# Which engine makes the last copy and issues the final store of a decode layer

## The chip, the cores and the metric

The kernel runs on one core of a Trainium2 chip. The metric is the device time of one execution in microseconds (us). The profile of an execution also gives a *span*, from the kernel's first recorded instruction to its last. The span is about 2 us shorter than the time. That difference matters in this study, and is called "time less span" below.

A ratio is the mean time of one kernel's fast runs over that of the kernel before's fast runs of the same rounds, so it is not quite the ratio of the medians that stand beside it.

The engines named below have these parts in this kernel. TensorE makes the matrix products, whose sums lie in the memory called PSUM. VectorE and ScalarE compute on elements and copy sums from PSUM to SBUF, the working memory. SyncE issues DMA transfers. A semaphore is a counter that an engine or a transfer raises and that another engine waits for. SPq and ACTq in the profile are the instruction queues of SyncE and ScalarE.

## The reference

The reference is one decode step of a transformer layer: four sequences, one token each, width 1024.

```python
x = A_x
h = x + _A_ref(_layernorm(x), A_k_cache, A_v_cache, A_wq, A_wo)   # attention, the last 2048 keys
h2 = h + _B_ref(_layernorm(h), B_w1, B_w3, B_w2)                   # silu(gate) * up, then w2
return h2                                                          # 4 x 1 x 1024, bf16
```

It reads 55.6 MB of weights and cache and writes 8 KB.

## The kernel before

All large loads are issued by SyncE in the order of a plan, through five buffers. `load_rows` cuts a tile into pieces, one load each. Each load takes the next of eight completion semaphores in turn ("lane" 0 to 7).

```python
def load_rows(src, n, r0, pieces):
    t = stream.tile([P, SLOT], BF16, tag="s")
    i = 0
    for m in pieces:
        nc.sync.dma_start(out=t[:, i * n : (i + m) * n], in_=src[:, (r0 + i) * n : (r0 + i + m) * n])
        i += m
    return [t[:, k * n : (k + 1) * n] for k in range(i)]

plan = (
    [("wq", load_rows, (wq_v, N_Q, c, [2, 2] if c == 0 else [4])) for c in range(0, KC, RQ)]
    # ... k, v, wo, w1 ...
    + [("w3", load_rows, (w3_v, N_F, c, [RQ])) for c in range(0, KC, RQ)]
    + [("w2", load_rows, (w2_v, D, 0, [16])), ("w2", load_rows, (w2_v, D, 16, [5, 4, 2, 1]))]
)
```

ScalarE issues five small loads of x at the start, then works as one of the two engines that copy out of PSUM:

```python
nc.scalar.dma_start(out=x_sb[:], in_=x_flat)
load_next(5)
# ...
for j in range(JG):                       # JG = 4
    nc.scalar.dma_start(out=x_q[QD * j : QD * (j + 1) : RS, :], in_=x_flat[:, j * CG : (j + 1) * CG])
```

The end of the kernel: 112 matmuls accumulate the last product as w2 arrives, VectorE casts the sum from PSUM to SBUF, and SyncE issues the store. Only 16 of the 128 partitions hold results.

```python
for i in range(IF):                       # IF = 28 rows of w2
    for j in range(JG):
        nc.tensor.matmul(y2_ps[QD * j : QD * (j + 1), :], lhsT=hgT[:, i, :],
                         rhs=loaded["w2"][i][:, j * CG : (j + 1) * CG], ...)
res = act.tile([P, CG], BF16)             # 128 x 256
nc.vector.tensor_copy(out=res[:], in_=y2_ps[:])
nc.sync.dma_start(out=out_flat.rearrange("b (j c) -> j b c", j=JG), in_=res[0:P:RS, :])
```

After that the compiler adds a wait of SyncE for all engines and all eight lanes, and two barriers.

Of the kernel before, what the change touches and what calls it, by code (L numbers as in the profile page):

```python
# [10 lines left out]
P = 128  # L11
# [8 lines left out]
def kernel(  # L20
# [13 lines left out]
    nc = tc.nc  # L34

    B, _, D = A_x.shape
    Hkv, Sk, Dh = A_k_cache.shape[1], A_k_cache.shape[2], A_k_cache.shape[3]
    Hq = A_wq.shape[1] // Dh
    REP = Hq // Hkv
    W = min(4096, max(256, Sk // 4))  # L40
    F = B_w1.shape[1]
    KC = D // P
    FC = F // P
    NK = W // P
    NSB = W // 512
    assert B == 4 and D == KC * P and F == FC * P and Hq * Dh == 4096
    assert Dh == P and W == NK * P and B * Hq == P and Hkv == 4
    eps = 1e-5
    qscale = float(Dh) ** -0.5
# [2 lines left out]
    out_flat = out.flatten_outer_dims()  # L52
# [14 lines left out]
    JG = 4  # L67
    QD = P // JG
    RS = QD // B
# [89 lines left out]
    for j in range(JG):  # L159
        nc.scalar.dma_start(  # L160
            out=x_q[QD * j : QD * (j + 1) : RS, :], in_=x_flat[:, j * CG : (j + 1) * CG]
# [7 lines left out]
    for c in range(2):  # L169
# [8 lines left out]
        out=xn[:], in0=x_sb[:], scalar1=mv[:, 0:1], scalar2=rstd[:, 0:1],  # L178
# [4 lines left out]
    for kc in range(KC):  # L183
# [15 lines left out]
        out=perm[:].rearrange("p (h dq) -> p h dq", dq=JG),  # L199
        in_=ident[:].rearrange("p (dq h) -> p h dq", dq=JG),  # L200
# [7 lines left out]
    for j in range(2, JG):  # L208
        nc.vector.tensor_tensor(
            out=same[:, 0, :], in0=same[:, 0, :], in1=ident[:, j * QD : (j + 1) * QD], op=ALU.add  # L210
# [24 lines left out]
    for r in range(REP):  # L235
        nc.tensor.transpose(out=qt_ps[:, r, :], in_=q_sb[:, r * Dh : (r + 1) * Dh], identity=ident[:])  # L236
    nc.vector.tensor_copy(
        out=qz[:, :, : Hkv * QD].rearrange("p b (g z) -> p b g z", g=Hkv)[:, :, :, :REP],
        in_=qt_ps[:].rearrange("p r (g x) -> p x g r", g=Hkv)[:, :B, :, :],
# [24 lines left out]
    for u, (b, n) in enumerate(units):  # L264
        k_v = loaded["k"][b].rearrange("p (j d) -> p j d", d=Dh)
        kT = ktpool.tile([P, NJ, P], BF16, tag="kT")
        for t in range(NJ // TB):
            kt_ps = psA.tile([P, TB, P], BF16, tag=f"kt{nt % 4}")
            for jj in range(TB):
                nc.tensor.transpose(  # L270
                    out=kt_ps[:, jj, :], in_=k_v[:, n * NJ + t * TB + jj, :], identity=ident[:]
# [23 lines left out]
        out=Pm[:].rearrange("q (c jq) -> q jq c", jq=NSB), in_=scores_ps[:].rearrange("q (jq c) -> q jq c", jq=NSB),  # L295
# [48 lines left out]
    y2_ps = psB.tile([P, CG], FP32, tag="y2")  # L344
    g_ps = psB.tile([P, 2, 512], FP32, tag="g")
    u_ps = psB.tile([P, 2, 512], FP32, tag="u")
    for i in range(IO):
# [33 lines left out]
        out=hn[:], in0=h1[:], scalar1=tot[:, 0:1], scalar2=rstd2[:, 0:1],  # L381
# [5 lines left out]
        out=hnT[:].rearrange("p k x -> p (k x)"), in_=hn[:].rearrange("q (c k) -> q k c", k=KC)  # L387
# [5 lines left out]
    def gate_up(kind, out_ps):  # L393
# [27 lines left out]
        out=hgT[:].rearrange("p i x -> p (i x)"),  # L421
        in_=hg[:].rearrange("q s c -> q (s c)").rearrange("q (c i) -> q i c", i=IF),
# [12 lines left out]
            )  # L435

    res = act.tile([P, CG], BF16)
    nc.vector.tensor_copy(out=res[:], in_=y2_ps[:])  # L438
    nc.sync.dma_start(out=out_flat.rearrange("b (j c) -> j b c", j=JG), in_=res[0:P:RS, :])


# [28 lines left out]
```

## Time and profile before

| | before |
|---|---|
| time | 139.43 us median (139.16 to 139.54, 6 runs) |
| span of the profiled run | 137.42 us |
| TensorE / VectorE / ScalarE busy | 52% / 26% / 21% |
| DMA | 55.6 MB, mean 406 GB/s |

These lines are from the page of the kernel before. The first two are the span and the busy time of each engine; the DMA line is the busy share of the 16 DMA engines in 40 slices of the span, in tenths; the queue lines give packets, MB and share of DMA time (q1 is SyncE's queue, q10 ScalarE's).

```profile
span 137.4 us, 2307 instructions
...
PE 71.2 (52%) x1045; PEld 45.2 (33%) x1045; DVE 36.3 (26%) x63; ACT 29.0 (21%) x28; POOL 1.6 (1%) x7
...
DMA  5999999999999999999999999999999999998950
...
q1 hardware_dynamic: 4724, 55.58, 95.4%
...
q10 hardware_dynamic: 40, 0.02, 0.0%
...
DMA 70%; PE 19%; ACT 6%; SPq 1%; DVE 1%; issue 1%; ACTq 0%
```

The DMA row is at 8 tenths or more from the second slice until the last two, and the last line, the chain of work that ended last, is 70% DMA. So the load stream bounds the kernel. Only what comes after the last load can shorten the time without making the stream faster.

The end of that chain, in order of time (start, length, what):

```profile
95.17 37.81 DMA t<-in_B_w_dram
...
133.02 1.04 PE y_ps L428 x9
...
134.09 0.42 DVE res L438
```

The timeline of the tail (start, length, engine, line, operation; in brackets how long the engine had been idle and what ended that):

```profile
133.02 1.02 PE L428 MATMUL y_ps<-t,hgT 128*32 128x256 bf16 x12 [0.32 <-DMA t<-in_B_w_dram]
...
134.09 0.42 DVE L438 CAST res<-y_ps 128x256 bf16<-128x256 f32 x1 [11.51 <-PE y_ps L428]
134.54 0.70 SPq L439 DMA_DIRECT2D out_dram<-res  x1
```

The instructions that touch res, with their durations in ns, and SyncE's waits for the copy and for the store's landing:

```profile
L438 DVE CAST res<-y_ps x1: 425/425/425, 134.1 to 134.1; 128x256 bf16<-128x256 f32 x1
L439 SPq DMA_DIRECT2D out_dram<-res x1: 697/697/697, 134.5 to 134.5; - x1
```

```profile
SPq L439 <- DVE res L438: 34.9, 1, 34.9
...
SPq L465 <- DMA out_dram<-res: 1.1, 1, 1.1
```

From the last matmul on, everything is serial. One thing follows another: copy 0.42 us, issue 0.70 us, landing about 1.1 us, and 1.07 us until the span ends.

For the cost of the copy on ScalarE, its own groups by shape give two durations (count, busy us, mean ns):

```profile
L276 ACT COPY kT<-kt_ps 128x1024 bf16<-128x1024 bf16 x16 | 15.8, 1014 | 12.0 <-PE kt_ps L270 12.0
...
L314 ACT CAST PT_sb<-pt_ps 128x512 bf16<-128x512 f32 x2 | 1.2, 585 | 2.0 <-PE pt_ps L308 2.0
```

### The profile page before, as it was taken

The page shows a single profiled execution, that of the slowest core. Times are in us where ns is not written, and L with a number is a line of the kernel's source. Part 1 is how long each engine was busy: PE and PEld are TensorE (multiplying, and loading weights), DVE is VectorE, ACT ScalarE, POOL GpSimd, SP SyncE. Part 2 cuts the span into 40 slices and gives each one's busy share as a digit, 9 for nine tenths or more (in the row PEclk, how much of TensorE's full clock was granted, in tenths as well). Part 3 has the DMA queues.
Part 4 walks back from the last instruction along what each step waited for, and adds up shares of the span by engine and source line. Part 5 has one row for each costly group of instructions (what it writes and reads, how often), then busy time and mean ns, then how long its engine had stood idle before and what let it go on. Part 6 is the DMA issues. An engine that isn't in the chain of part 4 may idle for free.

```text
span 137.4 us, 2307 instructions
## 1 busy us (share of the span) xinstructions
PE 71.2 (52%) x1045; PEld 45.2 (33%) x1045; DVE 36.3 (26%) x63; ACT 29.0 (21%) x28; POOL 1.6 (1%) x7
## 2 busy tenths in 40 slices
PE   0152304798989889100995579544090530802960
PEld 0110001175656565000894457221030210302830
DVE  6430000244444444601400300530003970160001
ACT  0400000155564646098610000000005000000000
POOL 4000000000000000000000000000000000000000
PEclk9999999999999999975555555558655586555555
DMA  5999999999999999999999999999999999998950
GB/s 155 444 402 520 391 391 444 420 429 444 405 440 392 421 421 414 423 495 476 401 391 424 453 428 397 459 467 401 409 459 439 426 409 430 448 458 359 420 217 2
DMA packets 4773, 55.74 MB, mean 406 GB/s; under 512 B 376, under 2 KB 408, under 8 KB 2716
## 3 DMA queue, kind: packets, MB, share of 16 engines
q1 hardware_dynamic: 4724, 55.58, 95.4%
q8 instruction: 8, 0.13, 0.3%
q10 hardware_dynamic: 40, 0.02, 0.0%
q14 instruction: 1, 0.01, 0.0%
HBM read 55.59 MB, written 0.01 MB: 405 GB/s over the span
## 4 chain that ended last, share of the span: by engine, by line
DMA 70%; PE 19%; ACT 6%; SPq 1%; DVE 1%; issue 1%; ACTq 0%
DMA t<-in_B_w_dram 54%; DMA t<-in_A_wq_dram 15%; PE kt_ps L270 9%; ACT kT L276 5%; PE scores_ps L255 5%; PE q_ps L222 3%; PE g_ps L398 2%; SPq L97 1%; PE y_ps L428 1%; DVE q_sb L232 1%; ACT q_sb L233 0%; DVE res L438 0%; PE qt_ps L236 0%; ACTq L276 0%
## 5 line engine op out<-in xcount | busy, mean ns | idle before, releaser
L276 ACT COPY kT<-kt_ps 128x1024 bf16<-128x1024 bf16 x16 | 15.8, 1014 | 12.0 <-PE kt_ps L270 12.0
L270 PE MATMUL kt_ps<-ident,t 128*128 128x128 bf16 x256 | 16.5, 219 | 0.0
L270 PEld LDWEIGHTS <-t 128*128 128x128 bf16 x256 | 14.4, 98 | 5.0 <-issue 4.9
L274 DVE COPY kT<-kt_ps 128x1024 bf16<-128x1024 bf16 x16 | 11.1, 692 | 15.2 <-PE kt_ps L270 15.2
L398 PEld LDWEIGHTS <-hnT 128*32 128x32 bf16 x128 | 5.5, 140 | 25.0 <-issue 22.7
L222 PE MATMUL q_ps<-t,xnT 128*4 128x512 bf16 x64 | 7.2, 615 | 12.0 <-DMA t<-in_A_wq_dram 12.0
L398 PE MATMUL u_ps<-t,hnT 128*32 128x448 bf16 x64 | 6.4, 576 | 10.6 <-DMA t<-in_B_w_dram 10.6
L255 PE MATMUL scores_ps<-kT,qz 128*32 128x512 bf16 x64 | 9.9, 609 | 3.1 <-ACT kT L276 3.1
L428 PE MATMUL y_ps<-t,hgT 128*32 128x256 bf16 x112 | 6.7, 415 | 7.6 <-DMA t<-in_B_w_dram 7.6
L398 PE MATMUL g_ps<-t,hnT 128*32 128x448 bf16 x64 | 6.3, 574 | 8.0 <-DMA t<-in_B_w_dram 8.0
L322 PE MATMUL OT_ps<-PT_sb,t 128*128 128x8 bf16 x256 | 7.4, 168 | 1.9 <-issue 1.7
L428 PEld LDWEIGHTS <-hgT 128*32 128x32 bf16 x112 | 4.8, 139 | 10.0 <-issue 5.5
L349 PE MATMUL y_ps<-t,o 128*32 128x256 bf16 x128 | 7.2, 418 | 1.7 <-DMA t<-in_A_wo_dram 0.9
L322 PEld LDWEIGHTS <-t 128*128 128x128 bf16 x256 | 7.3, 104 | 2.1 <-issue 2.0
L222 PEld LDWEIGHTS <-xnT 128*4 128x4 bf16 x64 | 2.0, 111 | 16.4 <-issue 16.1
L308 PE MATMUL pt_ps<-Dm,Pm 128*128 128x128 bf16 x16 | 1.9, 308 | 9.3 <-DVE Dm L301 9.3
L349 PEld LDWEIGHTS <-o 128*32 128x32 bf16 x128 | 5.1, 144 | 3.5 <-issue 1.2
L412 DVE RECIPROCAL eg<-eg 128x896 f32<-128x896 f32 x1 | 5.8, 5754 | 0.0
L232 DVE TENSOR_SCALAR q_sb<-q_ps 128x512 bf16<-128x512 f32 x1 | 0.7, 692 | 17.8 <-PE q_ps L222 17.8
L233 ACT ACTIVATE q_sb<-q_ps 128x512 bf16<-128x512 f32 x1 | 0.6, 597 | 21.4 <-DVE q_sb L232 21.4
L308 PEld LDWEIGHTS <-Pm 128*128 128x128 bf16 x16 | 1.6, 142 | 9.8 <-ACT Pm L294 9.8
L294 ACT ACTIVATE Pm<-scores_ps,nmax 128x2048 bf16<-128x2048 f32 x1 | 4.8, 4783 | 0.0
(67 smaller groups left out, 37.0 us busy)
## 6 DMA issues: line engine op xcount, KB each, us to landing
t<-in_B_w_dram SPq DMA_DIRECT2D x4, 3584.0 KB
t<-in_A_k_cache_dram SPq DMA_DIRECT2D x4, 2048.0 KB, 25.6
t<-in_A_v_cache_dram SPq DMA_DIRECT2D x4, 2048.0 KB, 33.0
t<-in_A_wo_dram SPq DMA_DIRECT2D x2, 4096.0 KB, 32.5
t<-in_A_wq_dram SPq DMA_DIRECT2D x2, 2048.0 KB, 9.6
t<-in_A_wq_dram SPq DMA_DIRECT2D x1, 4096.0 KB, 21.0
t<-in_B_w_dram SPq DMA_DIRECT2D x1, 4096.0 KB, 39.9
t<-in_B_w_dram SPq DMA_DIRECT2D x1, 1280.0 KB, 34.9
```

The lines of the kernel that those rows point to most:

```text
L222: nc.tensor.matmul(q_ps[QD * g : QD * g + B, hf * 512 : (hf + 1) * 512], lhsT=xnT[:, kc, :], rhs=wq_t[:, c0 : c0 + 512], start=(kc == 0), ...
L255: nc.tensor.matmul(scores_ps[QD * g : QD * (g + 1), n * 512 : (n + 1) * 512], lhsT=qz[:, b, g * QD : (g + 1) * QD], rhs=kT_v[:, g, :, :], ...
L270: nc.tensor.transpose(out=kt_ps[:, jj, :], in_=k_v[:, n * NJ + t * TB + jj, :], identity=ident[:])
L274: nc.vector.tensor_copy(out=kT[:, t * TB : (t + 1) * TB, :], in_=kt_ps[:])
L276: nc.scalar.copy(out=kT[:, t * TB : (t + 1) * TB, :], in_=kt_ps[:])
L294: nc.scalar.activation(out=Pm[:].rearrange("q (c jq) -> q jq c", jq=NSB), in_=scores_ps[:].rearrange("q (jq c) -> q jq c", jq=NSB), func=A ...
L308: nc.tensor.matmul(pt_ps[:, jj, :], lhsT=Pm[:, (jb * JPB + jj) * P : (jb * JPB + jj + 1) * P], rhs=Dm[:], start=True, stop=True)
L322: nc.tensor.matmul(OT_ps[:, b, g * REP : (g + 1) * REP], lhsT=v_t[:, g, j, :], rhs=PT_sb[:, j, g * QD + b * REP : g * QD + (b + 1) * REP], ...
L349: nc.tensor.matmul(y_ps[QD * j : QD * (j + 1), :], lhsT=o4[:, i, :, :].rearrange("p b s -> p (b s)"), rhs=loaded["wo"][i][:, j * CG : (j + ...
L398: nc.tensor.matmul(out_ps[QD * j : QD * (j + 1), hf, :HF], lhsT=hnT[:, k, :], rhs=loaded[kind][k][:, c0 : c0 + HF], start=(k == 0), stop=( ...
L412: nc.vector.reciprocal(out=eg[:], in_=eg[:])
L428: nc.tensor.matmul(y2_ps[QD * j : QD * (j + 1), :], lhsT=hgT[:, i, :], rhs=loaded["w2"][i][:, j * CG : (j + 1) * CG], start=False, stop=(i ...
```

## The change

The intent is to keep copy and store on one engine: ScalarE reads PSUM, and issues the store itself, so no other engine has to be told. (An assertion on a shape is rewritten as well, which changes no instruction.)

```diff
     res = act.tile([P, CG], BF16)
-    nc.vector.tensor_copy(out=res[:], in_=y2_ps[:])
-    nc.sync.dma_start(out=out_flat.rearrange("b (j c) -> j b c", j=JG), in_=res[0:P:RS, :])
+    nc.scalar.copy(out=res[:], in_=y2_ps[:])
+    nc.scalar.dma_start(out=out_flat.rearrange("b (j c) -> j b c", j=JG), in_=res[0:P:RS, :])
```

The built program differs in nothing else: VectorE loses one instruction, SyncE the store, ScalarE gains both, with no table load.

More of the change, by code (lines that the diff above doesn't have):

```diff
@@ L42 @@
     KC = D // P
-    FC = F // P
     NK = W // P
     NSB = W // 512
-    assert B == 4 and D == KC * P and F == FC * P and Hq * Dh == 4096
+    assert B == 4 and D == KC * P and F % P == 0 and Hq * Dh == 4096
     assert Dh == P and W == NK * P and B * Hq == P and Hkv == 4
```

## The prediction

> **What bounds the kernel.** The DMA load stream. The page has the 16 DMA engines 90% busy or more in nearly all of the 40 slices, at a mean of 406 GB/s for 55.6 MB. The chain that ended last is 70% DMA; its last links are a 37.8 us load that ends at 132.98 us, 1.04 us of y_ps matmuls, and the 0.42 us copy to res. TensorE is busy 52%, VectorE 26%, ScalarE 21%. The built program keeps the order of instructions on every engine except for the two moved ones, so nothing before the last matmul should change.
>
> **What moves: the tail.** After the last matmul everything is serial and critical (timeline of the tail, and the queue's waits; span 137.42 us):
>
> - last y_ps matmul ends, about 134.04; copy on VectorE 134.09 to 134.51 (0.425 us);
> - store issued by SyncE 134.54 to 135.24 (0.697 us);
> - SyncE's wait for the store to land: 1.1 us, to 136.35;
> - end of the program, 1.07 us: SyncE checks the remaining semaphores, the engines meet in two barriers.
>
> The change touches 0.425 + 0.03 + 0.697 = 1.15 us. If all of it vanished, the gain would be 0.8%: beyond 2% is out of reach.
>
> **Costs.**
> 1. Copy. ScalarE's PSUM to SBUF cast of 128x512 takes 585 ns, its copy of 128x1024 1014 ns: 0.84 ns an element (of different types), so 128x256 should take about 0.37 us (estimate), 0.05 less than VectorE. The Trainium skill, "ScalarE: Activation LUTs", section "What ACT_TABLE_LOAD costs", states 0.833 ns an element; these lines agree. The built program has no table load for the copy.
> 2. Hop. VectorE to SyncE took 0.03 us. ScalarE still waits on its own completion semaphore before it issues: 0.03 to 0.07 us, so "same engine" saves about nothing.
> 3. Issue. ScalarE's five issues took 0.56 to 0.68 us (four-row transfers); SyncE's unobstructed loads 0.33 to 0.64, its store 0.70. I expect 0.6 to 0.9 us on ScalarE: -0.1 to +0.2.
> 4. Flight. The same 8 KB goes through the same 16 DMA engines, idle by then. The Trainium skill, "DMA: Bandwidth & Descriptors", section "Issuing engines are not separate DMA queues", says that only sequencer issue time is saved. ScalarE's load of x_sb, issued at 0.74, had landed when its reader started at 2.40, so its queue isn't much slower. About 1.1 us again.
> 5. End. SyncE still checks the store's semaphore and the others: unchanged.
>
> Sum: -0.2 to +0.2 us, centre near 0. Runs of the kernel before spread by 0.38 us.
>
> **Predicted:** 139.4 us, 138.9 to 140.0 for 8 in 10. Faster by over 2%: 0.01; within 2%: 0.98; slower by over 2%: 0.01.
>
> **Signs.** Right if: the last load and the last y_ps matmul end within 0.5 us of before; a ScalarE copy of res of 0.35 to 0.42 us without a table load ahead; store issue on ScalarE's queue 0.6 to 0.9 us; landing wait near 1.1 us; last matmul to end of span 3.2 to 3.7 us. Wrong if the ScalarE copy starts late after y_ps, the issue takes over 1 us, or the landing takes longer.
>
> **What could make it wrong.** A slow issue on a queue unused since 4 us; a hidden table load; a different pace of the 55.6 MB stream, which moves the time by more than the change does.

## The result and the profile after

| | before | changed |
|---|---|---|
| time, median | 139.43 us (139.16 to 139.54, 6 runs) | 139.05 us (138.95 to 139.22, 6 runs) |
| ratio | | 0.9976 (95% 0.9963 to 0.9989): same at 2% |
| span of the profiled run | 137.42 us | 137.23 us |
| its time less span | 2.01 us | 1.78 us |

The same views after. The page: one instruction moved from DVE to ACT, and twenty packets from q1 to q10, which is the store (16 of 512 bytes, and four for its semaphore).

```profile
span 137.2 us, 2307 instructions
...
PE 69.0 (50%) x1045; PEld 44.8 (33%) x1045; DVE 36.0 (26%) x62; ACT 29.5 (21%) x29; POOL 1.6 (1%) x7
...
DMA  5999989999999999999899999999999999998950
...
q1 hardware_dynamic: 4704, 55.58, 95.5%
...
q10 hardware_dynamic: 60, 0.02, 0.1%
...
DMA 70%; PE 20%; ACT 5%; SPq 1%; issue 1%; DVE 1%; ACTq 0%
```

The timeline of the tail:

```profile
133.53 0.40 PE L427 MATMUL y_ps<-t,hgT 128*32 128x256 bf16 x4 [0.23 <-DMA t<-in_B_w_dram]
...
133.98 0.37 ACT L437 CAST res<-y_ps 128x256 bf16<-128x256 f32 x1 [28.91 <-PE y_ps L427]
134.39 0.61 ACTq L438 DMA_DIRECT2D out_dram<-res  x1
```

The instructions that touch res, and SyncE's wait for the landing:

```profile
L437 ACT CAST res<-y_ps x1: 372/372/372, 134.0 to 134.0; 128x256 bf16<-128x256 f32 x1
L438 ACTq DMA_DIRECT2D out_dram<-res x1: 615/615/615, 134.4 to 134.4; - x1
```

```profile
SPq L464 <- DMA out_dram<-res: 41.5, 1, 41.5
```

The last line needs care. It is 41.5 us now and was 1.1 us before, but the store doesn't take longer: SyncE no longer issues anything after its last load at 94.6 us, so its wait begins there. A wait is counted from when its engine became free, not from when the thing waited for began.

Adding up the records of the trace from the start of the copy to the end of the span gives the tail, term by term. "To first packet" runs from the end of the issue to the store's first DMA packet; "to SyncE" from there to SyncE's first record after the landing.

| us | copy | hop | issue | to first packet | to SyncE | to end of span | tail |
|---|---|---|---|---|---|---|---|
| before | 0.425 | 0.027 | 0.697 | 0.603 | 0.506 | 1.075 | 3.333 |
| changed | 0.372 | 0.030 | 0.615 | 0.641 | 0.511 | 1.075 | 3.244 |
| difference | -0.053 | +0.003 | -0.082 | +0.038 | +0.005 | 0 | -0.089 |

So the tail explains 0.09 us. The two spans differ by 0.19 us. The rest, 0.10 us, is the start of the copy: 134.09 against 133.98, although the last data packet of the load stream ended at 133.18 and 133.20. The windows of the last matmuls (stretch, us, busy time and count by engine, granted TensorE clock, DMA share, GB/s) show why, first before, then changed:

```profile
131.50:134.10 2.60, 2.06 (x28) 1.03 (x27) 0.01 (x1) 0.00 (x0) 0.00 (x0) 0.50 0.38 143
```

```profile
131.50:134.10 2.60, 1.43 (x28) 0.73 (x27) 0.00 (x0) 0.12 (x1) 0.00 (x0) 0.89 0.35 136
```

The granted clock at that moment was 0.50 in one profiled run and 0.89 in the other. The change doesn't touch TensorE, and the control of the experiments, whose instructions are those of the kernel before, had 0.85 in the same stretch. So nothing is to be made of this part.

The measured gain is 0.38 us in medians. Tail and clock together stay inside the span and make 0.19 us in this pair. Another 0.23 us lies outside the span: 139.43 - 137.42 = 2.01 us before, 139.01 - 137.23 = 1.78 us after. The prediction has no term for that, so the experiments are about it.

### The profile page after: what moved, and what is told of

The parts are those of the page before. It is cut to its first block, busy times and chain, and to the rows that moved or that the text cites. A ratio compares the mean times of both kernels' runs of the same rounds, so it can differ in the third digit from the quotient of the medians.

```text
span 137.2 us, 2307 instructions
## 1 busy us (share of the span) xinstructions
PE 69.0 (50%) x1045; PEld 44.8 (33%) x1045; DVE 36.0 (26%) x62; ACT 29.5 (21%) x29; POOL 1.6 (1%) x7
## 4 chain that ended last, share of the span: by engine, by line
DMA 70%; PE 20%; ACT 5%; SPq 1%; issue 1%; DVE 1%; ACTq 0%
DMA t<-in_B_w_dram 54%; DMA t<-in_A_wq_dram 15%; PE kt_ps L269 10%; PE scores_ps L254 5%; ACT kT L275 4%; PE q_ps L221 3%; SPq L96 1%; PE g_ps L397 1%; PE qt_ps L235 1%; DVE q_sb L231 1%; PE y_ps L427 0%; ACT res L437 0%; ACTq L275 0%
## 5 line engine op out<-in xcount | busy, mean ns | idle before, releaser
L269 PE MATMUL kt_ps<-ident,t 128*128 128x128 bf16 x256 | 17.9, 231 | 0.0
L269 PEld LDWEIGHTS <-t 128*128 128x128 bf16 x256 | 15.9, 104 | 4.9 <-issue 4.9
L397 PEld LDWEIGHTS <-hnT 128*32 128x32 bf16 x128 | 4.9, 128 | 25.2 <-issue 22.4
L427 PE MATMUL y_ps<-t,hgT 128*32 128x256 bf16 x112 | 5.8, 373 | 8.4 <-DMA t<-in_B_w_dram 8.4
L397 PE MATMUL g_ps<-t,hnT 128*32 128x448 bf16 x64 | 4.9, 465 | 9.0 <-DMA t<-in_B_w_dram 9.0
L321 PEld LDWEIGHTS <-t 128*128 128x128 bf16 x256 | 7.3, 104 | 3.3 <-issue 3.2
L348 PE MATMUL y_ps<-t,o 128*32 128x256 bf16 x128 | 6.1, 381 | 0.8 <-DVE o L337 0.8
L348 PEld LDWEIGHTS <-o 128*32 128x32 bf16 x128 | 4.5, 136 | 2.3 <-DVE o L337 1.0
```

The source lines that it names most:

```text
L269: nc.tensor.transpose(out=kt_ps[:, jj, :], in_=k_v[:, n * NJ + t * TB + jj, :], identity=ident[:])
L321: nc.tensor.matmul(OT_ps[:, b, g * REP : (g + 1) * REP], lhsT=v_t[:, g, j, :], rhs=PT_sb[:, j, g * QD + b * REP : g * QD + (b + 1) * REP], ...
L348: nc.tensor.matmul(y_ps[QD * j : QD * (j + 1), :], lhsT=o4[:, i, :, :].rearrange("p b s -> p (b s)"), rhs=loaded["wo"][i][:, j * CG : (j + ...
L397: nc.tensor.matmul(out_ps[QD * j : QD * (j + 1), hf, :HF], lhsT=hnT[:, k, :], rhs=loaded[kind][k][:, c0 : c0 + HF], start=(k == 0), stop=( ...
```

## The experiments

### Either half alone, a control, and the change again

The edits, against the kernel before: the first run changes the copy alone, the second the store's queue alone, the third only the assertion, the fourth is the changed kernel again.

```diff
 # e1_copy_only                                  # e2_queue_only
-nc.vector.tensor_copy(out=res[:], ...)           nc.vector.tensor_copy(out=res[:], ...)
+nc.scalar.copy(out=res[:], ...)                 -nc.sync.dma_start(out=out_flat...)
 nc.sync.dma_start(out=out_flat...)              +nc.scalar.dma_start(out=out_flat...)
```

> ScalarE makes the copy, SyncE keeps the store. Tail theory (only the durations of the tail count): copy 0.37 us in place of 0.425, store issue 0.70, landing as before; last copy's start to end of span 0.05 us shorter than before (3.28 against 3.33), time 139.3 to 139.4. Rival 'outside the span' (0.2 us of the measured 0.34 to 0.4 us lie outside the profiled span and belong to the queue that makes the store): time less span stays at 2.0 us here. Rival 'noise or build': the time is anywhere within 0.3 us of before, unrelated to the tail.

> VectorE makes the copy, ScalarE issues the store from its own queue. Tail theory: copy 0.425, issue 0.61 in place of 0.70, first packet 0.04 later after the issue; tail 0.04 shorter than before (3.29 against 3.33), time 139.3 to 139.4. Rival 'outside the span': time less span falls to 1.8 us as in the changed kernel, time 139.1 to 139.2. Rival 'noise or build': no relation.

> The kernel before with only the two lines of the assertion of the diff, which leave every engine's instructions as they were: a control. Tail theory and 'outside the span': ratio to before 1.000 within 0.1%, time less span 2.0 us. Rival 'noise or build': ratio off by 0.2% or so, as large as the change's 0.24%.

> The changed kernel again, beside the other three on one chip. Tail theory: 0.09 us faster than before (ratio 0.9994). 'Outside the span': 0.3 us faster again (ratio 0.9976), time less span 1.8 us. 'Noise or build': the ratio moves by 0.1% or more from the 0.9976 measured first.

Measured, means of five runs each and of nine of the kernel before, on one chip (spans of single runs are recorded to 0.1 us, so a mean span is good to a few hundredths):

| | time | ratio (95%) | span | time less span | tail of the profiled run |
|---|---|---|---|---|---|
| before | 139.42 | | 137.39 | 2.03 | 3.333 (first profile) |
| copy only | 139.38 | 0.9997 (0.9984 to 1.0009) | 137.24 | 2.14 | 3.279 |
| queue only | 139.32 | 0.9993 (0.998 to 1.0005) | 137.30 | 2.02 | 3.314 |
| control | 139.39 | 0.9998 (0.9985 to 1.001) | 137.36 | 2.03 | 3.336 |
| changed | 139.07 | 0.9976 (0.9962 to 0.9989) | 137.28 | 1.79 | 3.257 |

The lines for res with the copy alone and with the queue alone:

```profile
L437 ACT CAST res<-y_ps x1: 372/372/372, 133.9 to 133.9; 128x256 bf16<-128x256 f32 x1
L438 SPq DMA_DIRECT2D out_dram<-res x1: 692/692/692, 134.3 to 134.3; - x1
```

```profile
L437 DVE CAST res<-y_ps x1: 425/425/425, 133.9 to 133.9; 128x256 bf16<-128x256 f32 x1
L438 ACTq DMA_DIRECT2D out_dram<-res x1: 615/615/615, 134.4 to 134.4; - x1
```

In the tail the halves add up: -0.054 for the copy, -0.019 for the queue, about -0.08 for both. In the time they don't. The halves gain 0.04 and 0.10 us, both together 0.35 us. "Noise or build" falls with the control (0.9998) and with the repetition (0.9976 both times). "Outside the span belongs to the queue" falls with the queue alone: 2.02 us, not 1.8. The copy alone was expected to leave 2.0 us and gave 2.14 (2.11 to 2.18), which no theory had foreseen. Time less span is steady within a kernel (1.73 to 1.83 us in the five runs of the changed kernel, 1.98 to 2.17 us in the nine of before) and needs both halves.

### What sets the time outside the span?

Three theories were left. Perhaps VectorE and SyncE must both have fewer instructions; perhaps it matters which engine works late; or perhaps ScalarE's instruction stream counts. For the third, I counted all of ScalarE's records in each trace (compute, DMA issues, semaphore and drain records): before 54, copy only 55, queue only 56 (the issue, and a semaphore record because it waits for two things), changed 57.

```diff
 # f1_vector_early: the changed kernel, plus
+    scr = act.tile([P, 1], FP32)
+    nc.vector.memset(scr[:], 0.0)                           # beside the memset of eps_t
 # f2_scalar_three: the kernel before, plus, after rstd
+    scr = act.tile([B, 4], FP32)
+    for i in range(3):
+        nc.scalar.copy(out=scr[:, i : i + 1], in_=rstd[:])
 # f3_sync_one_more: the changed kernel, with
-        nc.scalar.dma_start(out=x_q[...])
+        (nc.sync if j == JG - 1 else nc.scalar).dma_start(out=x_q[...])
 # f5_vector_late: the changed kernel, plus, after the copy to res
+    scr = act.tile([P, 1], FP32)
+    nc.vector.tensor_copy(out=scr[:], in_=res[:, 0:1])
```

> The changed kernel with one more VectorE instruction near the start (a 128x1 memset). So far time less span is 2.03 us for before, 2.14 for copy only, 2.02 for queue only, 1.79 for the changed kernel. Theory 'count on VectorE and SyncE' (that time is the longest of several engines' and both VectorE and SyncE must lose their instruction): 2.0 us here. Theory 'late work' (what counts is whether VectorE or SyncE still works in the tail): 1.8 us. Theory 'ScalarE's stream' (only the length of ScalarE's stream counts): 1.8 us. Span 137.2 to 137.4 under all.

> The kernel before with three more ScalarE instructions (tiny copies) at 6 us; copy and store stay on VectorE and SyncE. 'ScalarE's stream': time less span 1.8 us, time 0.24 us below before. 'Count on VectorE and SyncE' and 'late work': 2.0 us, time as before.

> The changed kernel with one of the four early x_q loads issued by SyncE instead of ScalarE, so SyncE's stream is one longer and ScalarE's one shorter. 'Count on VectorE and SyncE': time less span 2.0 us. 'Late work': 1.8 us. 'ScalarE's stream': may move either way by up to 0.3 us.

> The changed kernel with one more VectorE instruction in the tail, a 128x1 copy out of res beside the store's issue, off the critical chain. 'Late work' and 'count on VectorE and SyncE': time less span 2.0 us. 'ScalarE's stream': 1.8 us. Span 137.2 to 137.4 under all.

Measured, means of four runs each, seven of before:

| | ScalarE records | time | ratio (95%) | span | time less span |
|---|---|---|---|---|---|
| before | 54 | 139.40 | | 137.37 | 2.03 |
| f1, VectorE early | 57 | 139.16 | 0.9982 (0.9966 to 0.9998) | 137.35 | 1.81 |
| f5, VectorE late | 57 | 139.09 | 0.9977 (0.9962 to 0.9992) | 137.33 | 1.77 |
| f3, one x_q load from SyncE | 56 | 139.29 | 0.9994 (0.9977 to 1.0011) | 137.28 | 2.02 |
| f2, copy and store as before, three more on ScalarE | 57 | 139.24 | 0.9987 (0.9972 to 1.0002) | 137.40 | 1.84 |

One more VectorE instruction, early or late, leaves the small value: both other theories fall. Three useless ScalarE copies at 6 us, with copy and store where they were, bring it to 1.84 us (1.80 to 1.90, against 1.98 to 2.09 for the kernel before). The ratio of the times alone, 0.9987, would not settle this, since its interval reaches 1; the time less span does. One ScalarE record taken away from the changed kernel brings back 2.02 us, as 56 gave before. (That run, f3, also gives SyncE a load more, so by itself it would fit the theory of VectorE and SyncE too; f2, with as many SyncE records as before, 45, and 1.84 us, does not.) So what moved outside the span goes with the number of ScalarE's records, not with the store.

### How does it go on?

```diff
 # h1_scalar_four, h2_scalar_seven: the kernel before, plus, after rstd
+    for i in range(4):   # or 7
+        nc.scalar.copy(out=scr[:, i : i + 1], in_=rstd[:])
```

> The kernel before with four more tiny ScalarE copies at 6 us. So far time less span goes by the records of ScalarE in the trace, whatever they are: 54 gives 2.03 us, 55 gives 2.14, 56 gives 2.02, 57 gives 1.77 to 1.84. Here 58. Theory 'period of four': 2.0 to 2.05 us again. Theory 'the longer the better': 1.6 us or less. Theory 'only three kernels by chance': anything.

> The kernel before with seven more tiny ScalarE copies at 6 us, 61 records. 'Period of four': time less span 1.8 us, as at 57. 'The longer the better': well below 1.7 us. 'Chance': anything.

The means of four runs were 2.10 us at 58 records and 1.78 us at 61; ratios 1.0004 (0.9985 to 1.0023) and 0.9985 (0.9968 to 1.0002). At 61 "period of four" was met. At 58, where it said 2.0 to 2.05 us, it was missed: the four runs were 1.86, 1.89, 2.30 and 2.36 us, two levels, where 54 records gave 1.96 to 2.17 us throughout. "The longer the better" falls. A plain period of four isn't shown, and what the device does in that time isn't either.

The views of the profile end with the span, but the packed traces hold some records beyond it, of semaphores and of DMA packets. The last semaphore event comes 1.90 us after the end of the span in the profiles with 54, 55, 57 and 61 ScalarE records, 2.06 us after it with 56, and 1.99 us with 58. So the 0.2 us between 54 and 57 records does not show even there. One difference does show: with 58 and 61 records, and in no other profile, an 8 KB packet of the kind "instruction" starts after the span, 2.11 us after its end with 58 (a run of the upper level, 139.66 - 137.25 = 2.41 us) and 1.31 us after it with 61. The kernels with 57 (f2), 58 and 61 differ only in the number of the small ScalarE copies (and the width of the tile they write to). A fetch of instructions is therefore an obvious candidate for the two levels, but there is one profile of each kernel and no run tests it; between 54 and 57 records no such packet follows the span.

### The end of the program

In the before and changed tails alike, 1.075 us pass from SyncE's first record after the landing to the end of the span. The trace shows SyncE checking semaphores in pairs there, about 0.065 us each, and it begins with lane 3, which is the store's. Lane 7 comes last. If the store were on lane 7, the first four checks could be done while it is still under way. Four more loads before it move it there.

```diff
 # h3_store_checked_last: the changed kernel, with
-        + [("w3", load_rows, (w3_v, N_F, c, [RQ])) ...]
-        + [("w2", load_rows, (w2_v, D, 0, [16])), ...]
+        + [("w3", load_rows, (w3_v, N_F, c, [RQ] if c == 0 else [2, 2])) ...]
+        + [("w2", load_rows, (w2_v, D, 0, [4, 4, 4, 4])), ...]
```

> The changed kernel with four more load pieces from SyncE (two halves of the last w3 load, four quarters of the first w2 load), which moves the store from the semaphore that SyncE checks first at the end to the one that it checks last; 57 ScalarE records as in the changed kernel. Theory 'the end is serial after the store': SyncE's four checks of about 0.065 us each are done before the store lands, so landing to end of span shrinks from 1.08 to about 0.82 us and span and time fall by 0.25 us against the changed kernel, to about 138.8. Rival: the checks only move and something else takes their place, or the extra load pieces cost as much on the load stream; time 139.1 or more.

Time 139.03 us median, ratio 0.9974 (0.9959 to 0.9989): no better than the change alone. But the tail did shrink. SyncE's semaphore checks, in the kernel before and in this run (count, durations, first and last start):

```profile
L465 SPq EVENT_SEMAPHORE  x7: 17/28/28, 136.3 to 137.4; - x7
```

```profile
L464 SPq EVENT_SEMAPHORE  x7: 17/28/28, 129.5 to 137.2; - x7
```

The first is now at 129.5 us, before the store; the tail is 2.989 us, of which 0.812 after the landing (was 1.075). The gain was lost ahead of it: over four runs the mean span was 137.25 us, against 137.28 for the change, though the tail was 0.26 us shorter. In the profile the last load packet ended at 133.48 us in place of 133.20 (133.36 in the control, so part of this can be scatter). SyncE issued its last load at 116.65 us in place of 94.21, and its waits for loads before it could issue a B-weight load grew:

```profile
SPq L96 <- DMA t<-in_B_w_dram: 27.5, 5, 8.1
```

In the changed kernel that line reads 3.9 us for one wait. In the trace of h3 the last five of SyncE's loads each wait for the semaphore of their own lane, that is, for an earlier load to land. That this is what delays the stream fits, but it was not tested by itself.

The lane can be moved the other way, with four loads *fewer*:

```diff
 # i1_best: the changed kernel, with
-    [("wq", load_rows, (wq_v, N_Q, c, [2, 2] if c == 0 else [4])) ...]
+    [("wq", load_rows, (wq_v, N_Q, c, [4])) ...]
-    for j in range(JG):
-        nc.scalar.dma_start(out=x_q[QD * j : QD * (j + 1) : RS, :], in_=x_flat[:, j * CG : (j + 1) * CG])
+    nc.scalar.dma_start(out=x_q[0:P:RS, :], in_=x_flat.rearrange("b (j c) -> j b c", j=JG))
+    for i in range(3):                                   # after rstd; keeps ScalarE at 57 records
+        nc.scalar.copy(out=scr[:, i : i + 1], in_=rstd[:])
```

> The changed kernel with four loads fewer and the same bytes: x_q in one load in place of four, the first wq tile in one in place of two. That gives the store the semaphore that SyncE checks last, as in the run before, without more pieces late in the load stream; three tiny ScalarE copies at 6 us take the place of the three x_q issues, so ScalarE again has 57 records. Theory 'the end is serial after the store, and the pieces cost the stream': the last load ends at 133.2 to 133.3 us as in the changed kernel, tail 2.99 us in place of 3.24, time less span 1.79 us, time 138.8. Rival 'something else always takes the place': span 137.2 and time 139.0 to 139.1.

```profile
133.90 0.37 ACT L437 CAST res<-y_ps 128x256 bf16<-128x256 f32 x1 [28.81 <-PE y_ps L427]
134.30 0.60 ACTq L438 DMA_DIRECT2D out_dram<-res  x1
```

```profile
L464 SPq EVENT_SEMAPHORE  x7: 17/28/28, 129.3 to 136.8; - x7
```

Time 138.86 us median (138.66 to 138.92, 5 runs), ratio 0.9959 (0.9945 to 0.9972). The last load packet ended at 133.22 us, the tail was 2.977 us, the mean span 137.04 us (changed: 137.28), the time less span 1.78 us. This beats both kernels: 0.55 us below before in the medians, 0.2 us below the change. The change was repeated on another chip, and the intervals of the two ratios overlap; but the kernel before had a mean of 139.42 us both beside the repeated change and here, and all five runs lie below the lowest of the change's eleven (138.95 us). Time, tail and last load are as expected. It is still within 2%.

## Why the prediction was right or wrong

The time, 139.05 us, lay in the range, and "within 2%" held. In part that was luck: the range had room for the scatter of the runs, and the sum of the terms alone, at most 0.2 us faster, would have missed. Point by point:

- **What bounds the kernel**: right. The stream's last packet ended at 133.18 and 133.20 us, and the change could reach only what follows.
- **Copy**: right. 0.372 us against the estimate of 0.37. Table load: none.
- **Hop**: right. 0.030 us on one engine against 0.027 between two. Keeping copy and store together saves no handover.
- **Issue**: right, at the low end: 0.615 us (0.60 to 0.62 in the runs with the store on ScalarE; 0.69 to 0.70 on SyncE).
- **Flight**: right in the main. From the end of the issue to SyncE's record it was 1.15 us against 1.11; 0.04 us of what the issue saved is spent before the first packet. The Trainium skill, "DMA: Bandwidth & Descriptors", section "Issuing engines are not separate DMA queues", says that DMAs run on the same 16 engines whichever engine starts them, and that starting them from several at once saves only issue time. Here one store moves and nothing runs beside it, but the trace agrees (-0.082 us of issue) and adds the +0.038 us.
- **End**: right inside the span, 1.075 us both times.
- **Sum**: "-0.2 to +0.2 us, centre near 0" was too narrow: medians moved by -0.38 us in the first runs, means by -0.35 us in the repetition. The step that failed is the one that treated the end of the kernel as unchanged and stopped at the end of the span. It silently took the 2 us of time beyond the span as fixed. In the repetition they went from 2.03 to 1.79 us, 0.24 of the 0.35 us; the rest is the tail (0.08) and scatter. The change has this effect because it raises ScalarE's records from 54 to 57: three idle copies have it too, and one record less takes it away. How the number of records does this is not known.
- **Signs**: last load within 0.02 us, copy 0.37 us, issue 0.61 us, last matmul to end of span 3.29 us (137.23 - 133.94): all as said. The "landing wait near 1.1 us" can't be read from the wait's line any more, since SyncE now waits from its last load on; the packets show it.

What stays open: why the number of ScalarE's records moves time outside the span, and why 58 records give two levels. The traces cover that time only by semaphore events and DMA packets, and these do not show the 0.2 us.

## What to carry to other kernels

Where a load stream bounds a kernel, list the serial tail term by term before moving an instruction in it: here the two halves of a "same engine" change were worth 0.05 and 0.02 us, and the order in which the end of the program checks its semaphores was worth 0.26 us of the tail. Compare the time with the span as well as the spans with each other, and run both halves of a change and a control: an effect of 0.2 us that needs both halves, and that three idle instructions reproduce, isn't the mechanism one had in mind. A tail that is made shorter by cutting loads into more pieces can be lost again in the stream, so look where the last load ends before crediting the tail.

## What the Trainium skill lacked or had wrong

- "Runtime: NRT & Kernel Launch", section "The ~15µs preamble/postamble breakdown", gives its stages one time each, and a total that depends on engine count and DMA setup. No page has it that time outside the kernel's span moves with the number of an engine's instructions: 2.03 us at 54 ScalarE records, 2.14 at 55, 2.02 at 56, 1.77 to 1.84 at 57, 1.78 at 61 (means), and single runs from 1.86 to 2.36 at 58.
- "DMA: Bandwidth & Descriptors", section "Issuing engines are not separate DMA queues", has neither an issue time nor a time to the first packet engine by engine for one and the same transfer. This store of 16 rows of 512 bytes took 0.69 to 0.70 us to issue on SyncE and 0.60 to 0.62 on ScalarE, and its first packet followed 0.60 us after the issue on SyncE and 0.64 to 0.65 on ScalarE.
- No page has the cost of the order in which the last wait of a program checks its semaphores: about 0.065 us a pair, 0.26 us when the store's comes first.
- "ScalarE: Activation LUTs", section "What ACT_TABLE_LOAD costs", states 186 ns + 0.833 ns an element with immediate scale and bias, which makes an estimate of 0.399 us for 256; the copy took 0.372 us. The copies out of PSUM here, 372 ns at 256 elements and 585 ns at 512, agree with the 0.83 ns an element but leave about 159 ns (an estimate from these two) beside it, less than the 186 stated.
